# Two groups of maxima in every second step: a new order of TensorE's work in a two-layer attention and GLU kernel

## The chip, the cores and the metric

The kernel runs on one core of one Trainium2 chip. The metric is the time of one execution on the device in microseconds (us), the median over several runs. The profile is one further execution, recorded instruction by instruction. The engines are TensorE (PE, whose weight loads are listed apart as PEld), VectorE (DVE), ScalarE (ACT), GpSimd (POOL) and SyncE (SP, which issues most of the transfers).

## The reference

A sequence of 2048 rows of 448 numbers goes through attention, a GLU, attention and a GLU again, each with a layer norm ahead of it and a sum with its own input behind it. Both attentions use the same weights, and so do both GLUs.

```python
def _A_ref(x, wq, wk, wv, wo):
    B, S, D = x.shape
    H = 16
    Dh = D // H
    q = (x @ wq).reshape(B, S, H, Dh).transpose(0, 2, 1, 3)
    k = x @ wk
    v = x @ wv
    scores = jnp.einsum("bhqd,bkd->bhqk", q, k) * (Dh ** -0.5)
    p = _softmax(scores, axis=-1)
    o = jnp.einsum("bhqk,bkd->bhqd", p, v)
    ...
def _B_ref(x, w_gate, w_up, w_down):
    h = _sigmoid(x @ w_gate) * (x @ w_up)
    return h @ w_down
...
x = x + _A_ref(_layernorm(x, axis=-1), A_wq, A_wk, A_wv, A_wo)
x = x + _B_ref(_layernorm(x, axis=-1), B_w_gate, B_w_up, B_w_down)
```

(The einsums of the GLU are written as matrix products here.) All 16 heads of 28 numbers share one key and one value of 28 numbers per row. D is 448, the GLU's inner width F is 1792.

## The kernel before, in words

**Split numbers.** Most products are made in 16-bit numbers: a value is split into a high part and the rest, and three products (high with high, high with rest, rest with high) are added in PSUM. A product with 448 rows is so a chain of 11 matmuls (`chain`, line 338).

**Units and steps.** The queries are handled in units of 128 rows, 16 units per layer. For a unit all 16 heads are worked on together, and the keys are taken in 16 steps of 128 rows. A step (variable `kt`) has these parts:

- S, `scores` (line 507): one of four groups of four heads; a matmul (line 510) of 512 columns writes a bank of PSUM, and ScalarE takes the exponential into a tile P (line 513).
- P, `pv` (line 516): the products of a step's four P tiles with the values, in four column strips of the array at once, added up over the 16 steps in a bank of its own (line 521). P is made for the step before.
- M, one call of the generator `mx_gen` (line 464). It works for a later unit: it finds each query's largest score, which is subtracted inside the score product. A call makes four matmuls in four row strips of the array at once (line 480), each into a bank of its own, and VectorE reduces each of the four banks to a maximum (line 484). After sixteen groups, the next call first reduces the sixteen results (lines 493 and 494), has TensorE transpose them (`fin`, line 499), has VectorE copy them (line 501), and has GpSimd's queue store them into the tile QS with the queries (line 502); then it makes the next unit's first group.
- F, `fill.slice` (line 767): a slice of filler. The filler is a list of generators, each of which issues one matmul at a time with an assumed cost in ns: projections of queries (`qgen`, 11 x 216 per group of heads) and the GLU of blocks of two units (`Block.bulk`, line 651). A slice first runs the deferred work that is due (`flush`), then issues matmuls until its budget is spent.
- X: side work (`tick`, line 536): the stages of a finished unit (`Block.tile`, line 557: one over the sums of the softmax, by way of DRAM; the output product `wo`, line 612; the layer norm), and the setting of the filler's rate.

**The order.** It is written out by hand in the last loop: `ORDER = "FSFSFSFSPXM"` for each step. Engines take their work in the order in which it is issued. The rate per step is the filler that is left divided by the steps until it is due; the four slices share it.

**The GLU.** `glu(f)` (line 655) handles two blocks of 128 inner columns: 22 matmuls into the bank `gp`, from which ScalarE makes the tanh `th` (line 665; the sigmoid is written by a tanh); 22 into the bank `up`; then VectorE forms (th + 1) x up (line 673), ScalarE copies this in 16 bits as h (line 676), the GLU's second activation, and VectorE makes the rest (line 677). Seven such groups and two `down` products (line 692, 42 matmuls each) make a block.

**Deferral.** `defer(fn, lag)` (line 66) puts an evacuation off until a later `flush`; the lag counts slices. `fps` (line 80) takes a bank and flushes first.

**Banks and buffers.** Scores, maxima and every product of the filler take their banks from one pool of seven; the eighth bank is that of `pv`. Tiles of SBUF have a number of buffers each: P eight, the GLU's h `HB` = 10. Ahead of the main loop, the h buffers hold the rows of x as they are loaded (`load_x0`).

The functions that the change touches follow with their line numbers.

Of the kernel before, what the change touches and what calls it, by code (L numbers as in the profile page):

```python
# [19 lines left out]
def interleaved_layers_kernel(ctx: ExitStack, tc: tile.TileContext, x, wq, wk, wv, wo, wg, wu, wd, out, layers=2):  # L20
# [9 lines left out]
    H, Dh = 16, 28  # L30
    NT, NB, G, KT, FC = S // 128, S // 512, H // 4, S // 128, F // 128
    U = NT
    TB, WB, HB = 2, 4, 10
    NBL = NT // TB
    EPS = 1e-5

# [29 lines left out]
    def defer(fn, lag=0):  # L66

        pend.append((now[0] + lag, fn))

    def flush(every=False):  # L70
        todo, pend[:] = pend[:], []
        for i, (due, fn) in enumerate(todo):
            if due > now[0] and not every:
                pend.append((due, fn))
            else:
                fn()
        if every and pend:
            flush(True)
# [77 lines left out]
    def prep_q():  # L156
        parts = wk1.tile([128, 4], F32, name="parts", bufs=1)
        for c in range(4):
            junk = wk1.tile([128, D], F32, tag="P", name="junq", bufs=8)
            squares(parts[:, c:c + 1], rq[:, c], junk)  # L160
        nc.vector.tensor_reduce(mxa[:, 2:3], parts, axis=AX.X, op=OP.add)
        nc.vector.memset(WQ[:, :, :, :, Dh:32], 0.0)
        yield
        yield from scales(mxa[:, 2:3], 1, pwa[:, 2:3], swa[:, 2:3])
        for c in range(4):
            r = rq[:, c].rearrange("p (h d) -> p h d", d=Dh)
            split(WQ[:, 0, c, :, 0:Dh], WQ[:, 1, c, :, 0:Dh], r, swa[:, 2:3])
            yield
        nc.vector.tensor_scalar(esc, pwa[:, 2:3], pwa[:, 0:1], None, op0=OP.mult)
        nc.vector.tensor_scalar(esc, esc, Dh ** -0.5 * 2.0 ** -14, None, op0=OP.mult)  # L170
# [336 lines left out]
    def scores(l, u, kt, g, P):  # L507
        assert ("m", l, u) in stored, (l, u, kt)
        s = psf.tile([128, 512], F32, tag=BANKS["s"], name="s", bufs=NBK[BANKS["s"]])
        nc.tensor.matmul(s, KK[l][0:96, 0, kt * 128:(kt + 1) * 128], QS[l, u][:, g].rearrange("p h n -> p (h n)"),  # L510
                         start=True, stop=True)
        p = wk1.tile([128, 512], F32, tag="P", name="P", bufs=8)
        nc.scalar.activation(p, s, AF.Exp, scale=esc)  # L513
        P.append(p)

# [32 lines left out]
    class Block:  # L548
# [8 lines left out]
        def tile(self, u):  # L557

            l, b = self.l, self.b
            t = u % TB  # L560
            v = {}

            def f0():
                v["o"] = PVS.pop((l, u))
                nc.sync.dma_start(sums[u % 2], v["o"][28:128:32])
                v["xr"] = wk1.tile([128, D], F32, tag="xr", name="xr", bufs=4)
                nc.sync.dma_start(v["xr"], x[0, u * 128:(u + 1) * 128] if l == 0 else x2d[u])
                return
                yield

            def fx():
                v["rc"] = wk1.tile([128, 16], F32, name="rc")
                nc.sync.dma_start(v["rc"], sums[u % 2].rearrange("g (a b) -> (g a) b", b=16))
                return
                yield

            def fy():
                nc.vector.reciprocal(v["rc"], v["rc"])
                return
                yield  # L580

            def fz():
                nc.sync.dma_start(sums[u % 2].rearrange("g (a b) -> (g a) b", b=16), v["rc"])
                return
                yield

            def fw():
                lb = v["lb"] = wk1.tile([128, 512], F32, name="lb", bufs=1)
                for g in range(G):
                    nc.sync.dma_start(lb[32 * g:32 * g + 32], sums[u % 2][g:g + 1].to_broadcast([32, 512]))  # L590
                return
                yield

            def fa():
                nc.gpsimd.tensor_tensor(v["lb"], v["o"], v["lb"], op=OP.mult)  # L595
                return
                yield

            def fb():
                oT = v["oT"] = wk1.tile([128, 2, 512], F16, name="oT")  # L600
                nc.scalar.copy(oT[:, 0], v["lb"])
                defer(lambda: nc.vector.tensor_tensor(oT[:, 1], v["lb"], oT[:, 0], op=OP.subtract))  # L602
                return
                yield

            def fc():
                need(1)
                p = fps([128, D], F32, "wo")
                n = 0
                for h in range(4):  # L610
                    for a, c in ((0, 0), (0, 1), (1, 0)):
                        nc.tensor.matmul(p, v["oT"][:, a, h * 128:(h + 1) * 128], WO[:, c, h], start=n == 0, stop=n == 11)  # L612
                        n += 1
                        yield C448

                def f():
                    nc.vector.scalar_tensor_tensor(self.x1[:, t], p, osc, v["xr"], op0=OP.mult, op1=OP.add)
                    v["ls"] = ln_stats(self.x1[:, t])[0]
                defer(f)

            def fd():
                if t == TB - 1:
                    self.load_w(0)
                    self.load_w(1)
                v["hl"] = ln_split(self.x1[:, t], *v["ls"], eng=nc.gpsimd)
                return
                yield

            def fe():
                if t == 0:  # L630
                    self.XT2 = wk1.tile([128, 7, TB * 128], F16, name="XT2")
                t7_dma(v["hl"], self.XT2, t)
                return
                yield

            def ff():
                self.fed += 1
                if self.fed == TB:
                    fill.add(self.bulk(), BULK)
                    if b == NBL - 1 and not self.last:  # L640
                        fill.add(qgen(l + 1, 1), G * QCH)
                return
                yield
            return (1, f0), (1, fx), (1, fy), (1, fz), (1, fw), (1, fa), (1, fb), (2, fc), (2, fd), (3, fe), (2, ff)
# [6 lines left out]
        def bulk(self):  # L651
# [3 lines left out]
            def glu(f):  # L655

                for j in range(2):
                    if f + j + 2 < FC:
                        self.load_w(f + j + 2)
                w = [self.wt.pop(f + j) for j in range(2)]  # L660
                gp = fps([128, 2, TB * 128], F32, "gp")
                for j in range(2):
                    yield from chain(gp[:, j], lambda a, c, k: w[j][:k, 0, a, c], lambda c, k: XT2[:k, c], C256, True)
                th = wk1.tile([128, 512], F32, tag="s2", name="th", bufs=3)
                defer(lambda: nc.scalar.activation(th, gp.rearrange("p j n -> p (j n)"), AF.Tanh, scale=gsc))  # L665
                up = fps([128, 2, TB * 128], F32, "up")
                for j in range(2):
                    yield from chain(up[:, j], lambda a, c, k: w[j][:k, 1, a, c], lambda c, k: XT2[:k, c], C256, True)
                h = wk1.tile([128, 2, 512], F16, name="h", bufs=HB)

                def ev():
                    t = th
                    nc.vector.scalar_tensor_tensor(t, th, 1.0, up.rearrange("p j n -> p (j n)"), op0=OP.add, op1=OP.mult)  # L673

                    def parts():
                        nc.scalar.activation(h[:, 0], t, AF.Copy, scale=2.0 ** -17)  # L676
                        defer(lambda: nc.vector.scalar_tensor_tensor(h[:, 1], t, 2.0 ** -17, h[:, 0], op0=OP.mult,  # L677
                                                                     op1=OP.subtract), 1)
                    defer(parts, 2)
                defer(ev)  # L680
                hs.append(h)

# [215 lines left out]
        nmx += 1  # L898

    early[0] = False  # L900
    ORDER = "FSFSFSFSPXM"
    MORE = (5, 10)
    FIRST = KT * TB + 16
    KEEP = 28000
# [1 line left out]
    for l in range(layers):  # L906
# [10 lines left out]
        while late:  # L917
            late.pop(0)[1]()
        fill.slice(QCH)
        prevP = None  # L920
        rate = 0.0
        for step in range(U * KT):
            u, kt = divmod(step, KT)
            P = []
            for o in ORDER:
                if o == "S":
                    scores(l, u, kt, len(P), P)
                elif o == "M":
                    for _ in range(1 + (u == 0 and kt in MORE)):
                        next(mx, None)  # L930
                elif o == "P":
                    if prevP is not None:
                        pv(*prevP)
                elif o == "X":
                    if u and kt == 1:
                        b = (u - 1) // TB
# [9 lines left out]
                    else:  # L946
                        rate = max(fill.left - KEEP, 0) / (U * KT - step)
                else:
                    fill.slice(rate / ORDER.count("F"))
            prevP = (l, u, kt, P)  # L950
        pv(*prevP)
        flush(True)
        later(*BLK[l, NBL - 1].tile(U - 1))
        if not final:
# [33 lines left out]
```

## Time and profile before

| | |
|---|---|
| median of 3 runs | 2359.96 us (2359.76 to 2361.04) |
| the profiled execution's own time | 2358.22 us |
| its span, from the first to the last instruction | 2356.4 us |
| mean granted TensorE clock | 0.985 |
| PE, DVE, ACT, POOL busy | 2239.1, 1635.5, 1559.2, 336.8 us |

The span is the time between the first and the last instruction; the execution's own time is 1.8 us more. A row of the timeline begins with the start and the length in us from the span's start, then engine, line, operation, the tiles written and read, the shape and the count; the bracket at its end gives the idle time ahead of it and what ended it. A row of the groups gives the line, engine, operation, tiles, shapes and count, then busy us and the mean ns of one, then the idle time before them with its releasers. A matmul's length on PE holds its way through the array, so that the next one starts before it ends: what one costs is read from start to start.

### The profile page before, as it was taken

What the parts mean: (1) busy time and instruction counts of PE and PEld (TensorE: products, weight loads), DVE (VectorE), ACT (ScalarE), POOL (GpSimd) and SP (SyncE); (2) the same over time, 40 slices, a digit from 0 to 9 for tenths busy, and PEclk for the clock granted to TensorE, in tenths of its full rate; (3) what the DMA queues carried; (4) which work ended last, traced back from release to release, by engine and by line L of the source; (5) the groups of instructions that cost most, each with busy time, mean ns of one, the idle gap of its engine ahead of it and who ended that gap; (6) DMA issues with size and microseconds to landing.
All of it is one profiled execution on the core that took longest, in us unless ns stands there. A gap on an engine that the chain in (4) does not pass through costs nothing.

```text
span 2356.4 us, 41206 instructions
## 1 busy us (share of the span) xinstructions
PE 2239.1 (95%) x15736; PEld 1003.2 (43%) x15736; DVE 1635.5 (69%) x2917; ACT 1559.2 (66%) x2598; POOL 336.8 (14%) x602
## 2 busy tenths in 40 slices
PE   5888899999999999999998989999999999999999
PEld 3322243444444444444572224444444444444456
DVE  6888787777777777773358877867676777777321
ACT  5588676776667677677413777767676776767751
POOL 5203763100110110001101011000000000000010
PEclk9799999999999999999998999999999999999999
DMA  3244652323313132333342112222231313223133
GB/s 114 65 126 124 201 190 81 90 73 98 96 58 109 58 93 70 94 92 78 96 139 53 27 49 92 87 78 83 62 103 58 98 55 101 76 82 94 57 111 119
DMA packets 208071, 213.88 MB, mean 91 GB/s; under 512 B 139952, under 2 KB 168304, under 8 KB 207872
## 3 DMA queue, kind: packets, MB, share of 16 engines
q1 hardware_dynamic: 202496, 196.36, 28.5%
q0 software_dynamic: 5376, 14.87, 1.8%
q8 instruction: 123, 2.02, 0.4%
q14 instruction: 76, 0.62, 0.1%
HBM read 175.37 MB, written 23.59 MB: 84 GB/s over the span
## 4 chain that ended last, share of the span: by engine, by line
PE 51%; DVE 5%; DMA 1%; ACT 1%; issue 0%; SPq 0%; POOL 0%; ACTq 0%; DVEq 0%; POOLq 0%
PE pv L521 12%; PE s L510 10%; PE dn L702 8%; PE gp L345 7%; PE up L345 7%; DVE mp L484 4%; PE mx L480 4%; PE wo L612 2%; PE qp L345 1%; ACT P L513 0%; DMA sums<-rc 0%; DMA KK<-ktl 0%; DMA rc<-sums 0%; DMA sums<-pvs 0%; DVE st L297 0%
## 5 line engine op out<-in xcount | busy, mean ns | idle before, releaser
L513 ACT ACTIVATE P<-s,esc 128x512 f32<-128x512 f32 x2048 | 1307.8, 690 | 509.2 <-PE s L510 492.1
L484 DVE TENSOR_REDUCE mp<-mx 128x1 f32<-128x512 f32 x2048 | 1267.2, 681 | 412.2 <-PE mx L480 408.1
L510 PE MATMUL s<-QS,KK 96*128 96x512 f16 x2048 | 761.1, 381 | 52.7 <-DVE mp L484 34.8
L345 PEld LDWEIGHTS <-wgu 128*128 128x128 f16 x4928 | 458.6, 98 | 241.3 <-issue 94.5
L521 PE MATMUL pv<-P,VV 128*32 128x512 f32 x4096 | 547.3, 607 | 0.0
L345 PE MATMUL up<-XT,wgu 128*128 128x256 f16 x2464 | 375.6, 272 | 0.8 <-DVE mp L484 0.8
L345 PE MATMUL gp<-XT,wgu 128*128 128x256 f16 x2464 | 375.2, 274 | 0.2
L702 PE MATMUL dn<-WD,h 128*128 128x448 f16 x1344 | 321.7, 352 | 0.0
L510 PEld LDWEIGHTS <-KK 96*128 96x128 f16 x2048 | 194.5, 97 | 172.1 <-issue 93.0
L480 PE MATMUL mx<-KK,QH 32*128 32x512 f16 x2048 | 223.2, 392 | 20.7 <-ACT QH L402 4.8
L480 PEld LDWEIGHTS <-QH 32*128 32x128 f16 x2048 | 53.5, 91 | 396.5 <-issue 378.1
L702 PEld LDWEIGHTS <-h 128*128 128x128 f16 x1344 | 124.1, 98 | 136.6 <-issue 22.6
L521 PEld LDWEIGHTS pv<-P,VV 128*32 128x32 f32 x4096 | 80.9, 108 | 204.4 <-issue 192.6
L595 POOL TENSOR_TENSOR lb<-pvs,lb 128x512 f32<-128x512 f32 x32 | 40.5, 1265 | 800.3 <-DMA lb<-sums 679.4
L676 ACT ACTIVATE h<-th 128x512 f16<-128x512 f32 x112 | 70.2, 627 | 86.4 <-DVE th L673 86.3
L345 PE MATMUL qp<-XT,WQ 128*128 128x512 f16 x352 | 114.5, 403 | 3.8 <-DVE mp L484 2.4
L673 DVE SCALAR_TENSOR_TENSOR th<-th,up 128x512 f32<-128x512 f32 x112 | 75.8, 677 | 59.0 <-PE up L345 46.5
L303 POOL TENSOR_SCALAR rs<-mv 128x1 f32<-128x1 f32 (+2 forms) x53 | 13.6, 256 | 686.4 <-DVE mv L298 682.9
L677 DVE SCALAR_TENSOR_TENSOR h<-th,h 128x512 f16<-128x512 f32 x112 | 77.7, 693 | 46.7 <-ACT h L676 46.7
L665 ACT ACTIVATE th<-gp,gsc 128x512 f32<-128x512 f32 x112 | 76.8, 685 | 47.7 <-PE gp L345 47.7
L612 PE MATMUL wo<-WO,oT 128*128 128x448 f16 x384 | 78.4, 353 | 0.3 <-DVE oT L602 0.2
L345 PEld LDWEIGHTS <-WQ 128*128 128x128 f16 x352 | 34.2, 101 | 64.2 <-issue 41.1
(126 smaller groups left out, 834.3 us busy)
## 6 DMA issues: line engine op xcount, KB each, us to landing
wgu<-wgu_d SPq DMA_DIRECT2D x224, 512.0 KB
QS<-qd SPq DMA_DIRECT2D x384, 32.0 KB
lb<-sums SPq DMA_DIRECT2D x128, 64.0 KB
xr<-in_A_x_dram SPq DMA_DIRECT2D x32, 224.0 KB
qd<-qst POOLq DMA_DIRECT2D x28, 256.0 KB, 2.7
wgu_d<-sgu POOLq DMA_DIRECT2D x14, 512.0 KB, 3.8
QH<-qd SPq DMA_DIRECT2D x28, 128.0 KB
x2d<-x SPq DMA_DIRECT2D x16, 224.0 KB
```

The source lines that it names most:

```text
L345: nc.tensor.matmul(ps, a, b, start=n == 0, stop=n == 10)
L480: nc.tensor.matmul(ps[h], qh[32 * h:32 * h + 32, g], KK[l][32 * h:32 * h + 32, 1, kb * 512:(kb + 1) * 512], start=True, stop=True, tile_po ...
L484: nc.vector.tensor_reduce(mp[:, g, h, kb:kb + 1], ps[h], axis=AX.X, op=OP.max)
L510: nc.tensor.matmul(s, KK[l][0:96, 0, kt * 128:(kt + 1) * 128], QS[l, u][:, g].rearrange("p h n -> p (h n)"), start=True, stop=True)
L513: nc.scalar.activation(p, s, AF.Exp, scale=esc)
L521: nc.tensor.matmul(v[32 * g:32 * g + 32], VV[l][:, kt], P[g], start=kt == 0, stop=kt == KT - 1, tile_position=(0, 32 * g))
L612: nc.tensor.matmul(p, v["oT"][:, a, h * 128:(h + 1) * 128], WO[:, c, h], start=n == 0, stop=n == 11)
L665: defer(lambda: nc.scalar.activation(th, gp.rearrange("p j n -> p (j n)"), AF.Tanh, scale=gsc))
L673: nc.vector.scalar_tensor_tensor(t, th, 1.0, up.rearrange("p j n -> p (j n)"), op0=OP.add, op1=OP.mult)
L676: nc.scalar.activation(h[:, 0], t, AF.Copy, scale=2.0 ** -17)
L677: defer(lambda: nc.vector.scalar_tensor_tensor(h[:, 1], t, 2.0 ** -17, h[:, 0], op0=OP.mult, op1=OP.subtract), 1)
L702: nc.tensor.matmul(p, hs[f // 2][:, a, o:o + 128], WD[:, f, c], start=n == 0, stop=n == 3 * FC - 1)
```

## The change

From a unit's second on, and when the filler's rate is over 800 ns per step at the start of a pair of steps, the pair is issued as "FSFSMPMFSFSX" and "FSFSFSFSX": both steps' groups of maxima and the products of the two steps before it (P empties a list) stand in its first step. Otherwise the order stays "FSFSFSFSPXM". Each M is preceded by a flush. The GLU's second activation is put off by four slices and not by two. P has twelve buffers and not eight, h eight and not ten, and the 16-bit attention output oT one and not two.

```diff
-    TB, WB, HB = 2, 4, 10
+    TB, WB, HB = 2, 4, 8
...
-        p = wk1.tile([128, 512], F32, tag="P", name="P", bufs=8)
+        p = wk1.tile([128, 512], F32, tag="P", name="P", bufs=12)
...
-                oT = v["oT"] = wk1.tile([128, 2, 512], F16, name="oT")
+                oT = v["oT"] = wk1.tile([128, 2, 512], F16, name="oT", bufs=1)
...
-                    defer(parts, 2)
+                    defer(parts, 4)
...
-    ORDER = "FSFSFSFSPXM"
+    FULL = ("FSFSMPMFSFSX", "FSFSFSFSX")
+    POOR = ("FSFSFSFSPXM", "FSFSFSFSPXM")
+    ENOUGH = 800
...
-        prevP = None
+        pend_p = []
         rate = 0.0
         for step in range(U * KT):
             u, kt = divmod(step, KT)
             P = []
-            for o in ORDER:
+            if kt % 2 == 0:
+                pair = FULL if u and rate > ENOUGH else POOR
+            order = pair[kt % 2]
+            for o in order:
                 if o == "S":
                     scores(l, u, kt, len(P), P)
                 elif o == "M":
+                    flush()
                     for _ in range(1 + (u == 0 and kt in MORE)):
                         next(mx, None)
                 elif o == "P":
-                    if prevP is not None:
-                        pv(*prevP)
+                    while pend_p:
+                        pv(*pend_p.pop(0))
...
-                    fill.slice(rate / ORDER.count("F"))
-            prevP = (l, u, kt, P)
-        pv(*prevP)
+                    fill.slice(rate / order.count("F"))
+            pend_p.append((l, u, kt, P))
+        while pend_p:
+            pv(*pend_p.pop(0))
```

More of the change, by code (lines that the diff above doesn't have):

```diff
@@ L158, in prep_q @@
         for c in range(4):
-            junk = wk1.tile([128, D], F32, tag="P", name="junq", bufs=8)
+            junk = wk1.tile([128, D], F32, tag="P", name="junq", bufs=12)
             squares(parts[:, c:c + 1], rq[:, c], junk)
```

## The prediction

> **What bounds the kernel now.** I read the busy shares first, then two stretches of the busy time by window, then the groups of instructions, then single steps in the timeline. The page's first part:
>
> ```profile
> PE 2239.1 (95%) x15736; PEld 1003.2 (43%) x15736; DVE 1635.5 (69%) x2917; ACT 1559.2 (66%) x2598; POOL 336.8 (14%) x602
> ```
>
> PE is at 95%, but that is a mean. The busy time by window separates two stages of layer 1: the first units, with little filler, and a unit in which filler is plentiful.
>
> ```profile
> 1260.00:1320.00 60.00, 54.69 (x288) 14.16 (x290) 52.35 (x91) 36.71 (x62) 3.26 (x5) 0.94 0.06 18
> 1500.00:1565.40 65.40, 64.73 (x442) 26.80 (x440) 45.91 (x80) 44.14 (x70) 4.64 (x10) 1.00 0.22 64
> ```
>
> After the window and its length stand PE, PEld, DVE, ACT, POOL, the clock, the DMA share and GB/s. At 1260 DVE leads (52.35 of 60). At 1500 PE is busy 64.73 of 65.40 us, DVE 70%, ACT 67%: there the order on PE alone sets the time, and a gap on PE is lost. Part of one such step, to the filler behind a group of maxima (mx):
>
> ```profile
> 1506.24 0.38 PE L510 MATMUL s<-QS,KK 96*128 96x512 f16 x1
> 1506.46 0.49 PE L345 MATMUL up<-XT,wgu 128*128 128x256 f16 x3
> ...
> 1508.10 0.38 PE L510 MATMUL s<-QS,KK 96*128 96x512 f16 x1
> 1508.41 1.07 PE L521 MATMUL pv<-P,VV 128*32 128x512 f32 x8
> 1509.41 0.40 PE L480 MATMUL mx<-KK,QH 32*128 32x512 f16 x4
> 1509.74 0.61 PE L345 MATMUL up<-XT,wgu 128*128 128x256 f16 x4
> ```
>
> I call filler F, a score S, a step's products with the values P, a group of maxima M, and count from start to start: S to F 0.22 (1506.24 to 1506.46), S to P 0.31, P to M 1.00, M to F 0.33. S, S is 0.62 apart ((1508.10 - 1506.24) / 3). So S costs 0.09 more ahead of P than ahead of F, and M, as long as S in columns, 0.11 more: each change between full array, four column strips (P) and four row strips (M) costs about 0.1.
>
> **The change, part by part.** *Order.* A pair of steps is SP, PM, MF twice: 2 x (0.31 + 1.00 + 0.33) = 3.28. Now it has S to M, M to P, P to P, P to M, M to F, and one S to F more. P to P comes from its second half:
>
> ```profile
> 1677.19 0.61 PE L521 MATMUL pv<-P,VV 128*32 128x512 f32 x4
> 1677.73 0.40 PE L480 MATMUL mx<-KK,QH 32*128 32x512 f16 x4
> 1678.06 0.55 PE L702 MATMUL dn<-WD,h 128*128 128x448 f16 x2
> 1678.45 0.38 PE L510 MATMUL s<-QS,KK 96*128 96x512 f16 x1
> 1678.67 0.73 PE L702 MATMUL dn<-WD,h 128*128 128x448 f16 x3
> 1679.24 0.38 PE L510 MATMUL s<-QS,KK 96*128 96x512 f16 x1
> ...
> 1680.93 1.06 PE L521 MATMUL pv<-P,VV 128*32 128x512 f32 x8
> 1681.82 0.22 PE L499 MATMUL mt<-id,m 128*16 128x128 f16 x1
> ```
>
> The last four of P start 0.54 ahead of M, so the first half takes 1.00 - 0.54 = 0.46, and P ahead of P 0.92. S to M and M to P stand nowhere; without a switch they were 0.22 each, with two switches 0.42 each; I take the nearest rows, S to P 0.31 and M to F 0.33. New pair: 0.31 + 0.33 + 0.92 + 1.00 + 0.33 + 0.22 = 3.11. It saves 0.17 (0.37 to -0.03 by the bounds). The Trainium skill, "TensorE: Matmul & The Clock Gate", Single matmul latency, gives a warm matmul a fixed part of 398 cycles at 2.4 GHz; an estimate from that page is 0.17 us for a switch that hides none of it, so that by it M to P would be 0.07 dearer, 15 us in 208 pairs.
>
> How many pairs: the rate is the filler left over the steps left. With one block it is (14 x 22 x 110 + 2 x 42 x 190) / 32 = 1557, over 800; with only projections of queries (at most 28512 / 48 = 594) it is under. The first block is fed at the end of the third unit, so units 3 to 15 of both layers are filled: 2 x 13 x 8 = 208 pairs. 208 x 0.17 = **-35**.
>
> *Attention's output product* stands between P and M now:
>
> ```profile
> 1533.17 2.44 PE L612 MATMUL wo<-WO,oT 128*128 128x448 f16 x12
> 1535.54 0.40 PE L480 MATMUL mx<-KK,QH 32*128 32x512 f16 x4
> ```
>
> 2.37 for twelve: one more switch, 0.1. In a filled pair it stands behind S, before F, with none: 26 x 0.1 = **-3**.
>
> *The maxima's end.* Three groups are drawn ahead (one before unit 0, two extra in it), so the sixteenth group for the next unit is M of step 12. The call after it, step 13's, begins with the last reduction (m32, m16) and its transpose mt on PE. In the new order both are the two M of one pair. In between lie 0.33 + 0.92 + 0.89 (P to mt, 1680.93 to 1681.82) = 2.14. On DVE:
>
> ```profile
> 1678.15 2.48 DVE L484 TENSOR_REDUCE mp<-mx 128x1 f32<-128x512 f32 x4 [1.74 <-PE mx L480]
> 1680.55 0.67 DVE L710 SCALAR_TENSOR_TENSOR x<-dn,dsc,x 128x448 f32<-128x448 f32 x1
> 1681.14 0.21 DVE L493 TENSOR_REDUCE m<-mp 128x16 f32<-128x64 f32 x1
> 1681.38 0.17 DVE L494 TENSOR_SCALAR m<-m 128x16 f16<-128x16 f32 x1
> ```
>
> ```profile
> 947.03 0.17 DVE L494 TENSOR_SCALAR m<-m 128x16 f16<-128x16 f32 x1
> 947.26 0.09 PEld L499 LDWEIGHTS <-m 128*16 128x16 f16 x1 [1.20 <-DVE m L494]
> ```
>
> From M's start: 0.42 to the first reduction (1677.73 to 1678.15), 2.40 until the next operation starts, 0.24 for m32, then 0.23 from m16 to mt's weights: 3.29. PE waits 3.29 - 2.14 = 1.15, with everything behind it in its order. Units 3 to 14 of two layers: 24 x 1.15 = **+28**; with one of DVE's 0.67 us evacuations ahead of the group 24 x 1.8 = 43.
>
> *Banks.* Scores, maxima and filler share seven banks. That a full pool stops PE is shown in an early unit:
>
> ```profile
> 200.56 0.40 PE L480 MATMUL mx<-KK,QH 32*128 32x512 f16 x4
> 200.88 0.61 PE L510 MATMUL s<-QS,KK 96*128 96x512 f16 x2
> 201.73 0.70 PE L510 MATMUL s<-QS,KK 96*128 96x512 f16 x2 [0.24 <-DVE mp L484]
> ```
>
> ```profile
> 201.00 2.47 DVE L484 TENSOR_REDUCE mp<-mx 128x1 f32<-128x512 f32 x4
> ```
>
> Four banks of M, an open filler chain and two S make seven; the third S starts 0.11 after the first reduction's end (201.00 + 2.47 / 4 = 201.62). Now the new M1: it follows S2 by 0.31, and S1 by 0.93. ScalarE's rows:
>
> ```profile
> 1505.22 0.68 ACT L665 ACTIVATE th<-gp,gsc 128x512 f32<-128x512 f32 x1
> 1506.66 2.61 ACT L513 ACTIVATE P<-s,esc 128x512 f32<-128x512 f32 x4 [0.76 <-PE s L510]
> ```
>
> An exponential starts 0.42 after its S (1506.24 to 1506.66), follows another by 0.65 (2.61 / 4) and holds the bank until its end, 0.69 (the groups' row below). Set M1 at 0. S1's exponential ends at -0.93 + 0.42 + 0.69 = 0.18 at best, S2's later: both banks are taken, one holds the open chain, four are left, just what M1 needs. But eight S now come 0.62 apart from S3 of the pair before (start -4.65), and exponentials 0.65 apart: undisturbed S8's ends at -4.65 + 0.42 + 5 x 0.65 + 0.69 = -0.29. One other activation (0.65) among them makes that 0.36: M1's fourth matmul waits until 0.36 + 0.11, **0.45**. Two make it 1.01, and S7's 0.36: **1.1**. Before, P's 1.00 lay between S4 and M: S4's exponential ended 1.31 - 0.42 - 0.69 = 0.20 before M, and one running late left M five banks.
>
> How often: each GLU group of 44 matmuls puts th and h on ScalarE.
>
> ```profile
> L513 ACT ACTIVATE P<-s,esc 128x512 f32<-128x512 f32 x2048 | 1307.8, 690 | 509.2 <-PE s L510 492.1 <-PE gp L345 0.3 <-PE dn L702 0.2
> ...
> L665 ACT ACTIVATE th<-gp,gsc 128x512 f32<-128x512 f32 x112 | 76.8, 685 | 47.7 <-PE gp L345 47.7
> L673 DVE SCALAR_TENSOR_TENSOR th<-th,up 128x512 f32<-128x512 f32 x112 | 75.8, 677 | 59.0 <-PE up L345 46.5 <-ACT P L513 6.4 <-PE gp L345 6.1
> L676 ACT ACTIVATE h<-th 128x512 f16<-128x512 f32 x112 | 70.2, 627 | 86.4 <-DVE th L673 86.3
> ```
>
> With 1557 / 110 = 14 matmuls a step, gp and up (22 each) take 6.2 slices of F each. h is issued four slices after up's evacuation, so the next th follows it by about two: they fall into the same chain in six of the eight places, one alone in two. Mean (6 x 1.1 + 2 x 0.45) / 8 = 0.94 a group. Of the 112 groups 2 x 6 x 7 = 84 run beside maxima in filled pairs: 84 x 0.94 = 79. I take 0.85, as a slice may leave the next chain unopened: **+71**; bounds 0 (banks fall free in time) and 84 x 1.3 = 109 (a bank was bound ahead to the wrong tile). In the down product S come 0.79 apart (1678.45 to 1679.24), more than 0.65: nothing piles up, 0.
>
> *The rest at nothing:* h's later start is hidden while PE waits for nothing of it (its 86.3 us of waiting are ScalarE's own); twelve buffers for P are needed, not a gain; the flush before M only reorders DVE's work, within 5 us either way where DVE leads. Eight buffers ahead in the prologue:
>
> ```profile
> L794 SPq DMA_DIRECT2D xr<-in_A_x_dram x16: 327/405/594, 0.7 to 30.4; - x16
> L816 DVE BATCH_NORM_STATS2 st<-xr x16: 594/614/628, 3.3 to 43.2; 128x6 f32<-128x448 f32 x16
> ```
>
> The last load leads its use by 12.8; two tiles less (2 x 39.9 / 15 = 5.3) leave 7.5, and the first load needed 2.6. No cost, at most 5. *Queues:* a call of M also issues the next unit's loads (SP) and mr's store (POOL, busy 4.64 of 65.40). They now come up to a step earlier, and the stages of X on the other side of them; the next unit's scores read them two steps later or more, so nothing waits. Behind M1's waiting matmul stand P, P and all of PE's order; ScalarE and DVE go on with what they have, so a wait is not passed on to the next pair.
>
> **Sum.** -35 - 3 + 28 + 71 = +61 on the profiled run's 2358.2 us (span 2356.4): 2419. The runs' median lies 1.7 higher: **2421**.
>
> **Rivals.** A, the forecast, with its own range: banks 34 to 109, 2384 to 2460. The Trainium skill, "TensorEngine Tiling (Array Packing)", Restrictions and Gotchas, warns that row tiling raises PSUM pressure, since row tiles write different banks; the 0.24 us wait at 201.73 agrees.
> B, the faster side: banks fall free in time, because the flush ahead of M and the later h put th and h into ScalarE's gap behind M1. It decides where S8's exponential ends before M1, one activation less in the chain. Then -35 - 3 + 28 = -10: 2350. For it: ScalarE idles a third of the unit. Against: seven of the eight slices lie in or beside the chain.
> C: the transpose too finds DVE done: -38, 2322. Against it the 3.29 against 2.14.
> D: M to P and S to M cost two switches each, so the order saves nothing: 2421 + 35 = 2456.
> E: only double disturbances stop PE, half of the 71: 2386; or the change hardly bites, as few pairs exceed 800: 2360.
>
> **How the numbers follow.** A and the upper part of E 0.60, D 0.07, E's rest 0.08, B 0.20, C 0.05. Range 2345 to 2460: it takes in A, D, E and most of B, and leaves out C and the tails, 0.2. About 0.2% (4.7 us) is what a measurement here can tell from no change. Faster: most of B, and C, 0.24; same: 0.07; slower: 0.69.
>
> **What would show it.** In the filled units: P in groups of 16 matmuls, M to P near 0.33; once per unit a gap of about 1.15 before mt, put down to m (L494); gaps inside M's four matmuls of 0.4 to 1.1 put down to the exponential (L513), one or two per GLU group and none in the down product. If M's matmuls start without a gap, the bank term is wrong and the time is B's; if mt waits for nothing, C's. PE's busy share in filled units should fall from 99% to about 94%.

## The result and the profile after

The changed kernel takes 2393.27 us (median of 4 runs, 2391.18 to 2395.06), the kernel before 2359.86: a ratio of 1.0141, 95% interval 1.0123 to 1.0158. It is slower by 33 us; 61 were forecast, with a range of 2345 to 2460. The profiled execution's span is 2389.4 us (2356.4 before).

Busy time by window of the changed kernel, for the same two stretches as before (early units; one filled unit). The columns are the window, its length, PE, PEld, DVE, ACT, POOL, the clock, the DMA share and GB/s:

```profile
1260.00:1320.00 60.00, 52.36 (x273) 15.33 (x270) 49.59 (x88) 26.21 (x48) 6.61 (x13) 0.89 0.17 48
1505.90:1571.90 66.00, 63.88 (x468) 31.18 (x468) 48.58 (x83) 45.50 (x75) 4.94 (x10) 1.00 0.24 68
```

(The first window now holds the end of layer 0's tail, as everything is later by 19 us.) This filled unit takes 66.0 and not 65.4 us (in layer 1 the units now take 66.0 and 66.7 in turn), and PE is busy 63.88 of it, 97% where it was 99%. PE's instructions are the same; it waits more. The groups by line show where. First the kernel before, then the changed one; the columns are busy us and the mean ns of one, then the idle time ahead of them and what ended it:

```profile
L521 PE MATMUL pv<-P,VV 128*32 128x512 f32 x4096 | 547.3, 607 | 0.0
...
L480 PE MATMUL mx<-KK,QH 32*128 32x512 f16 x2048 | 223.2, 392 | 20.7 <-ACT QH L402 4.8 <-DMA KK<-ktl 4.6 <-DVE mp L484 4.1
```

```profile
L521 PE MATMUL pv<-P,VV 128*32 128x512 f32 x4096 | 511.9, 609 | 0.0
L480 PE MATMUL mx<-KK,QH 32*128 32x512 f16 x2048 | 271.0, 391 | 34.4 <-ACT P L513 7.9 <-DVE mp L484 5.1 <-ACT QH L402 4.8
```

The products P lose 35 us of busy time, because two groups now follow one another without a drain between them. The maxima M gain 48: their four matmuls, which started 3 ns apart, now often stand apart. A matmul here is drawn 0.39 long, so that a wait shorter than this inside a group shows as busy time and not as idle time; it must be read from start to start. (This is also why PE's busy share stands at 97% and not at the 94% that the prediction named as a sign.)

A pair without a wait, from the changed kernel's timeline of PE:

```profile
1527.46 0.38 PE L510 MATMUL s<-QS,KK 96*128 96x512 f16 x1
1527.78 0.39 PE L480 MATMUL mx<-KK,QH 32*128 32x512 f16 x4
1528.10 1.92 PE L521 MATMUL pv<-P,VV 128*32 128x512 f32 x16
1529.96 0.40 PE L480 MATMUL mx<-KK,QH 32*128 32x512 f16 x4
1530.29 0.61 PE L345 MATMUL gp<-XT,wgu 128*128 128x256 f16 x4
```

From start to start: S to M 0.32, M to P 0.32, both groups of P 1.86, M to F 0.33. With the extra S to F of 0.22 that is 3.05 against 3.28 before: 0.23 saved per pair, where 0.17 was forecast.

The transpose of the maxima, once a unit (PE's timeline, then VectorE's):

```profile
1568.49 0.40 PE L480 MATMUL mx<-KK,QH 32*128 32x512 f16 x4
1568.81 1.92 PE L521 MATMUL pv<-P,VV 128*32 128x512 f32 x16
1571.91 0.22 PE L499 MATMUL mt<-id,m 128*16 128x128 f16 x1 [1.18 <-DVE m L494]
```

```profile
1568.91 2.48 DVE L484 TENSOR_REDUCE mp<-mx 128x1 f32<-128x512 f32 x4 [1.51 <-PE mx L480]
1571.43 0.22 DVE L493 TENSOR_REDUCE m<-mp 128x16 f32<-128x64 f32 x1
1571.68 0.18 DVE L494 TENSOR_SCALAR m<-m 128x16 f16<-128x16 f32 x1
```

The transpose starts 3.42 after the unit's last group M, just behind the reductions; PE stands still for 1.18. In the 24 filled units with maxima the idle time ahead of the transpose is 1.05 to 1.39, 28.2 us in all; in the same units of the kernel before it is 2.8.

A pair in which M waits (PE's timeline, then ScalarE's):

```profile
1519.26 0.38 PE L510 MATMUL s<-QS,KK 96*128 96x512 f16 x1
1519.57 0.39 PE L480 MATMUL mx<-KK,QH 32*128 32x512 f16 x3
1520.15 0.37 PE L480 MATMUL mx<-KK,QH 32*128 32x512 f16 x1 [0.19 <-ACT th L665]
1520.45 1.93 PE L521 MATMUL pv<-P,VV 128*32 128x512 f32 x16
```

```profile
1515.36 2.49 ACT L513 ACTIVATE P<-s,esc 128x512 f32<-128x512 f32 x4 [2.30 <-PE s L510]
1517.75 0.62 ACT L676 ACTIVATE h<-th 128x512 f16<-128x512 f32 x1
1518.27 1.26 ACT L513 ACTIVATE P<-s,esc 128x512 f32<-128x512 f32 x2
1519.41 0.69 ACT L665 ACTIVATE th<-gp,gsc 128x512 f32<-128x512 f32 x1
1519.98 1.28 ACT L513 ACTIVATE P<-s,esc 128x512 f32<-128x512 f32 x2
```

Three matmuls of M start at 1519.57, the fourth 0.58 later, 0.05 after the tanh's end at 1520.10. On ScalarE h stands after the fourth of eight exponentials and th after the sixth, two slices apart, and the last two exponentials end only at 1521.26. I counted, at each waiting matmul of M in ten filled units of each layer, the banks between their first write and their last read: 133 matmuls in 103 of 320 groups waited, 51.0 us in all. At 114 of them, with 49.4 us, all seven banks were held. In the same units of the kernel before, three matmuls of M waited, 1.0 us in all.

### The profile page after: what moved, and what is told of

Its sections match the earlier page's. It is cut to its first block, busy times and chain, and to the rows that moved or that the text cites. A ratio compares the mean times of both kernels' runs of the same rounds, so it can differ in the third digit from the quotient of the medians.

```text
span 2389.4 us, 41472 instructions
## 1 busy us (share of the span) xinstructions
PE 2240.1 (94%) x15736; PEld 1048.5 (44%) x15736; DVE 1641.9 (69%) x2917; ACT 1530.9 (64%) x2598; POOL 338.9 (14%) x602
## 4 chain that ended last, share of the span: by engine, by line
PE 67%; DVE 14%; ACT 9%; issue 3%; DMA 2%; SPq 1%; POOL 1%; ACTq 0%; POOLq 0%; DVEq 0%
PE s L510 14%; PE pv L521 14%; PE dn L702 11%; DVE mp L484 10%; PE up L345 9%; PE gp L345 9%; ACT P L513 7%; PE mx L480 6%; PE wo L612 3%; PE qp L345 2%; DVE x L617 1%; DVE st L297 1%; ACT th L665 1%; ACT h L676 0%; DMA sums<-rc 0%
## 5 line engine op out<-in xcount | busy, mean ns | idle before, releaser
L513 ACT ACTIVATE P<-s,esc 128x512 f32<-128x512 f32 x2048 | 1290.3, 694 | 579.7 <-PE s L510 564.2
L345 PEld LDWEIGHTS <-wgu 128*128 128x128 f16 x4928 | 469.6, 98 | 222.4 <-issue 58.2
L521 PE MATMUL pv<-P,VV 128*32 128x512 f32 x4096 | 511.9, 609 | 0.0
L480 PE MATMUL mx<-KK,QH 32*128 32x512 f16 x2048 | 271.0, 391 | 34.4 <-ACT P L513 7.9
L510 PEld LDWEIGHTS <-KK 96*128 96x128 f16 x2048 | 196.3, 97 | 150.9 <-issue 66.7
L521 PEld LDWEIGHTS pv<-P,VV 128*32 128x32 f32 x4096 | 103.3, 109 | 280.0 <-issue 271.5
L617 DVE SCALAR_TENSOR_TENSOR x<-wo,osc,xr 128x448 f32<-128x448 f32 x32 | 21.9, 684 | 84.8 <-PE wo L612 84.8
## 6 DMA issues: line engine op xcount, KB each, us to landing
qd<-qst POOLq DMA_DIRECT2D x28, 256.0 KB, 2.6
```

The lines of the kernel that those rows point to most:

```text
L345: nc.tensor.matmul(ps, a, b, start=n == 0, stop=n == 10)
L480: nc.tensor.matmul(ps[h], qh[32 * h:32 * h + 32, g], KK[l][32 * h:32 * h + 32, 1, kb * 512:(kb + 1) * 512], start=True, stop=True, tile_po ...
L521: nc.tensor.matmul(v[32 * g:32 * g + 32], VV[l][:, kt], P[g], start=kt == 0, stop=kt == KT - 1, tile_position=(0, 32 * g))
```

## The experiments

The theory (T) is the prediction's: the order saves switches, and loses more to two new waits, the transpose's for VectorE and the first group's for a bank. Each ratio below is to the kernel before on the same chip, where its median was 2357.7 to 2360.2 us; a difference in us between two experiments is one of medians, and some of these were taken on different chips.

**1. The transpose one group later.**

```diff
-    LT = 1
+    LT = 2
```

> The changed kernel with one edit: the transpose of the maxima (L499) is issued one group of maxima later. Theory T (two new waits outweigh the saved mode switches: the transpose waits for VectorE, and the first group of maxima waits for PSUM banks): in the changed kernel's trace the idle time before the transpose in filled units is 1.05 to 1.18 us, 24 times; 22 of these go (the last unit of each layer has no later group), so 2393 - 26 = 2367. Rival R1 (the flush, the lag and the buffers cost the time, not the order): the wait was idle time that something else would have filled, 2393 within 5. Rival R2 (the long run of scores makes ScalarE late and the products wait for exponentials): within 5 of 2393 too.

Measured: 2365.82 us, ratio 1.0025 (1.0015 to 1.0034): 27.5 less than the changed kernel. In its timeline of PE the transpose stands at the head of the next pair's first group and waits for nothing:

```profile
1561.26 0.38 PE L510 MATMUL s<-QS,KK 96*128 96x512 f16 x1
1561.57 0.22 PE L499 MATMUL mt<-id,m 128*16 128x128 f16 x1
1561.73 0.40 PE L480 MATMUL mx<-KK,QH 32*128 32x512 f16 x4
```

The wait was worth its full length, as T has it; R1 and R2 expected no change. (The transpose of each layer's last unit still waits 1.18; the 22 waits that are gone make 25.8 us in the trace.) 5.6 us above the kernel before are left.

**2. A slice of filler ahead of the first group.**

```diff
-    FULL = ("FSFSMPMFSFSX", "FSFSFSFSX")
+    FULL = ("FSFSFMPMSFSX", "FSFSFSFSX")
```

> The changed kernel with one slice of filler moved from behind the pair's second group of maxima to ahead of its first (FSFSFMPMSFSX). The number of mode switches stays. T: ScalarE has 0.42 us more before the first group asks for four banks, so a single activation in the chain no longer stops it, and two stop it by 0.7 and not 1.1; the gaps inside the groups of maxima, 51 us in 20 units of the changed kernel (103 groups of 320), fall to a third: 2393 - 40 = 2353. R1: 2393 within 5, as flush, lag and buffers stay. R2: the run of eight scores stays, so the products would still wait: 2393 within 10.

Measured: 2385.82, ratio 1.0114 (1.0097 to 1.0131): 7.5 less, not 40. The direction is T's, the size is not. Counted from start to start in the same 20 units, the gaps in M fell from 51.0 to 35.6, and those ended by an exponential from 26.1 to 14.4. But the next score now followed the second group directly, 0.32 behind its start and without filler between, while the banks of M were held: start to start, the steps around it (M to S and S to F in place of M to F and F to S) grew by some 13 us. Seven banks were short at one place or at the other.

**3. The old order with the rest of the change.**

```diff
-    ENOUGH = 800
+    ENOUGH = 10 ** 9
```

> The changed kernel with the filled pairs switched off (the rate is never over the threshold), so that the order of the kernel before stands everywhere and only the flush before M, the longer lag and the numbers of buffers are left of the change. T: 2360 within 5. R1: near 2393. R2: 2360 within 5.

Measured: 2362.7, ratio 1.0016 (1.0007 to 1.0025). In the old order, flush, lag and buffers cost about 2.5 us (2 to 6 by the interval of the ratio); the rest of the 33 comes with the order. R1 falls.

**4. Both of 1 and 2.**

```diff
-    LT = 1
+    LT = 2
...
-    FULL = ("FSFSMPMFSFSX", "FSFSFSFSX")
+    FULL = ("FSFSFMPMSFSX", "FSFSFSFSX")
```

> Both edits: the transpose one group later and the filler slice ahead of the first group of maxima. T: the savings add up, 2393 - 26 - 40 = 2327, faster than the kernel before by 1.4%. R1 and R2: no faster than 2380.

Measured: 2369.02, ratio 1.0040 (1.0027 to 1.0053). No faster than experiment 1 alone: what the filler slice gained beside a waiting transpose it did not gain without it; why is not shown. My sum was wrong; the gain of 7.5 was not one that adds up.

**5. The second activation on GpSimd.** On top of experiment 1:

```diff
-                        nc.scalar.activation(h[:, 0], t, AF.Copy, scale=2.0 ** -17)
+                        nc.gpsimd.tensor_scalar(h[:, 0], t, 2.0 ** -17, None, op0=OP.mult)
...
-                                                                     op1=OP.subtract), 1)
+                                                                     op1=OP.subtract), 4)
```

> The kernel with the transpose one group later, and GLU's second activation (h) made by GpSimd and not ScalarE, its rest three slices later still. T (in a filled pair the first group of maxima finds all seven banks held, by exponentials that run late and by others): one of the two activations that delay the exponentials is gone; of the changed kernel's 51 us of gaps inside the groups of maxima in 20 filled units 26 were ended by an exponential and 8 by the tanh, and about half of these 34 should go: 2366 - 20 = 2346. Rival R3 (the gaps come from the exponentials' own number, eight scores in a row, whatever else ScalarE does): 2366 within 5.

Measured: 2344.11, ratio 0.9934 (0.9918 to 0.9951): 22 less than experiment 1, and faster than the kernel before. Its groups by line (the profiled execution took 2350.51 us):

```profile
L480 PE MATMUL mx<-KK,QH 32*128 32x512 f16 x2048 | 256.0, 393 | 26.7 <-DVE mp L484 5.9 <-ACT QH L402 4.8 <-DMA KK<-ktl 4.2
...
L676 POOL TENSOR_SCALAR h<-th 128x512 f16<-128x512 f32 x112 | 167.6, 1497 | 664.3 <-DVE th L673 663.0
```

GpSimd takes 1.5 us (its spans in the profile are rough) for what took ScalarE 0.63, but it has the time. M's busy time falls from 271.0 to 256.0 (experiment 1 alone left it at 270.4), and the counted gaps from 51.0 to 31.1; those ended by an exponential or the tanh are some 16 of these, where they were 34.5. The number of scores in a row is unchanged, so R3 falls: it matters what else ScalarE has between them. (The edit also puts h's rest off by three more slices; the two parts were not run one without the other.)

**6. Each step its own group, the products in pairs.**

```diff
-    FULL = ("FSFSMPMFSFSX", "FSFSFSFSX")
+    FULL = ("FSFSPMFSFSX", "FSFSMFSFSX")
```

> The changed kernel with the pair ordered FSFSPMFSFSX and FSFSMFSFSX: the products of two steps still stand together, but each step has its own group of maxima, half a pair apart. A pair then has five kinds of switches: S to P 0.31, P to P 0.41, P to M 0.525, M to F 0.317, S to M 0.313, M to F 0.317 = 2.19, where the order before has 2.30: -0.11 x 208 = -23. T: the transpose and its last group are nearly four us apart again, as before, so it does not wait; the first group follows two steps' products, 1.4 us after the last score, and finds its banks; the second follows two scores that came after a pause of ScalarE: few gaps, at most 10. 2360 - 23 + 5 = 2342. R3: the second group of maxima waits like the changed kernel's first: 2360 - 23 + 30 = 2367.

Measured: 2378.41, ratio 1.0082 (1.0067 to 1.0097). A miss, by two errors of mine in reading the order. From the first group to the second there is not half a pair but four scores with their filler:

```profile
1554.12 0.39 PE L480 MATMUL mx<-KK,QH 32*128 32x512 f16 x4
...
1557.20 0.38 PE L510 MATMUL s<-QS,KK 96*128 96x512 f16 x1
1558.02 0.22 PE L499 MATMUL mt<-id,m 128*16 128x128 f16 x1 [0.43 <-DVE m L494]
```

From 1557.20 the next group could start 0.31 later, 3.4 after 1554.12, which is too soon for the reductions: the transpose still waits, by 0.43 and 0.88 in turn in layer 1 and by 1.1 to 1.3 in most filled units of layer 0, 20.6 us in all against the changed kernel's 28.2. And the second group follows four scores, not two, so it lacks banks (37.7 us of counted gaps in 20 units, against 51.0), while the first, behind the products, waits nowhere. R3's number is the nearer one: its second group waits, and the transpose's waits, which it did not have, come on top.

**7 and 8. Six banks.** The same edit in the changed kernel and in the kernel before:

```diff
-    NBK = {"f": 7, "s": 2, "m": 3}
+    NBK = {"f": 6, "s": 2, "m": 3}
```

> The changed kernel with six banks for scores, maxima and filler and not seven. T: now even an undisturbed pair lacks a bank when its first group asks for four (two scores, one chain), and waits some 0.3 us for an exponential; disturbed pairs wait for one exponential more (0.65): 190 pairs x 0.4 = 76 more, 2393 + 76 = 2469, nearly all of it as gaps inside groups of maxima. If banks were not what the gaps are for: 2393 within 10.

> The kernel before with six banks. T: a group of maxima follows the products there, when the scores' banks have come free, so that the filled units lose little (under 5 us in all); the early units of a layer, where VectorE leads, lose at most 15: 2360 + 10 = 2370. If any bank less costs every order the same: as much as the changed kernel loses.

Measured, one run each: 2521.96 for the changed kernel (129 more) and 2470.72 for the kernel before (111 more). I expected the old order to lose a tenth of that, and it does not. Groups by line, first the changed kernel with six banks, then the kernel before with six:

```profile
L510 PE MATMUL s<-QS,KK 96*128 96x512 f16 x2048 | 765.9, 381 | 74.7 <-DVE mp L484 47.5 <-ACT P L513 23.3 <-DVE x L617 1.8
...
L480 PE MATMUL mx<-KK,QH 32*128 32x512 f16 x2048 | 332.3, 392 | 61.8 <-ACT P L513 35.6 <-DVE mp L484 6.3 <-ACT th L665 4.0
```

```profile
L510 PE MATMUL s<-QS,KK 96*128 96x512 f16 x2048 | 767.5, 382 | 109.4 <-DVE mp L484 88.0 <-ACT P L513 14.5 <-DVE ktl L376 2.1
...
L480 PE MATMUL mx<-KK,QH 32*128 32x512 f16 x2048 | 240.7, 395 | 24.9 <-DVE mp L484 8.0 <-DMA QH<-qd 4.4 <-DMA KK<-ktl 3.8
```

The old order, too, lives on all seven, but is short at another place: its scores behind M wait for the reductions (88.0 us), while the new order's M wait for the exponentials (busy 332.3, idle ahead of it 61.8). Counted in the 20 units, the gaps inside M grew from 51 to 119 us in the new order and from 1 to 13 in the old one. The pair of runs supports that banks are what M waits for; it does not show that the old order has a bank to spare.

**9. The lag back at two**, in the changed kernel.

```diff
-                    defer(parts, 4)
+                    defer(parts, 2)
```

> The changed kernel with the second activation's lag back at two slices. T: the activation is then issued while VectorE is still at the reductions ahead of its product, so ScalarE stands still for it and the exponentials behind it are later: more gaps inside the groups of maxima, 2393 + 15 = 2408. R1 (the longer lag is part of the loss): 2380 or less.

Measured: 2403.93, ratio 1.0195 (1.0179 to 1.0210), 10.7 more (13 by the two ratios). The waits of ScalarE, first of the changed kernel, then of this one, in total us, times and the longest:

```profile
ACT h L676 <- DVE th L673: 44.7, 19, 3.2
```

```profile
ACT h L676 <- DVE th L673: 74.9, 43, 9.3
```

Counted start to start, the gaps in the first groups grew from 45.9 to 54.8 us in the 20 units, as T has it. The longer lag is a gain inside the new order; R1 falls again.

**10. The control: the second activation on GpSimd in the old order.** Its order is unchanged.

```diff
-                        nc.scalar.activation(h[:, 0], t, AF.Copy, scale=2.0 ** -17)
+                        nc.gpsimd.tensor_scalar(h[:, 0], t, 2.0 ** -17, None, op0=OP.mult)
...
-                                                                     op1=OP.subtract), 1)
-                    defer(parts, 2)
+                                                                     op1=OP.subtract), 4)
+                    defer(parts, 4)
```

> Control: the kernel before, its order unchanged, with GLU's second activation on GpSimd and the longer lags. T: in the filled units of the kernel before no group of maxima waits for a bank, so a lighter ScalarE gains nothing: 2360 within 4. If the second activation's move is a gain by itself (R4), as much as it gained in the new order: 2360 - 22 = 2338.

Measured: 2352.84, ratio 0.9975 (0.9966 to 0.9985). A gain of 6 where I expected none within 4, and far from R4's 22. So about 16 of experiment 5's 22 belong to the new order. Counted from transpose to transpose, the filled units give 0.35 and 0.21 us each in the two layers, some 7 in all. From start to start, 4 of the 6 us in 20 units lie between a filler matmul and the score behind it; a score that waits less for its bank would do that, but this is not shown.

**11. All three edits.** On top of experiment 5:

```diff
-    FULL = ("FSFSMPMFSFSX", "FSFSFSFSX")
+    FULL = ("FSFSFMPMSFSX", "FSFSFSFSX")
```

> The transpose later, the second activation on GpSimd, and the slice of filler ahead of the first group of maxima. T: the filler slice took 15 of 51 us of gaps at the first group and gave half of that back at the score behind the second; with fewer gaps left (31 us in 20 units) it can take at most 6: 2344 - 4 = 2340, the same within 5.

Measured: 2346.82, ratio 0.9957 (0.9940 to 0.9973): the same as experiment 5 within the intervals.

**12. The later transpose in filled pairs alone.** On top of experiment 5:

```diff
-    LT = 2
+    LT = [1]
...
-            late.append([LT, fin])
+            late.append([LT[0], fin])
...
+                LT[0] = 2 if pair is FULL else 1
```

Its reason is a row of the waits of experiment 1 (total us, times, longest):

```profile
PE s L510 <- DMA QS<-mr: 5.9, 4, 2.0
```

> The kernel with the later transpose and the second activation on GpSimd, where the transpose is put off only in filled pairs. Putting it off everywhere made four scores in the early units wait 5.9 us in all for the transposed maxima's transfer (DMA QS<-mr); early units have the old place back. T: 2344 - 6 = 2338, 0.9% faster than the kernel before. If those waits were covered by VectorE's lead in the early units: 2344 within 3.

Measured: 2346.29, ratio 0.9948 (0.9934 to 0.9961): no gain over experiment 5. The number is that of the second case, but its reason is not what the traces show. PE's waits, first of experiment 5, then of this one:

```profile
PE s L510 <- DMA QS<-mr: 5.8, 4, 2.0
...
PE mt L499 <- DVE m L494: 2.4, 2, 1.2
```

```profile
PE mt L499 <- DVE m L494: 7.1, 9, 2.1
...
PE s L510 <- DMA QS<-mr: 2.5, 2, 2.0
```

The scores wait 3.3 us less for the transfer, and the early units' transposes, back in their old place, wait 4.7 us more for VectorE: the wait moved from the score to the transpose.

## Why the prediction was right, point by point

The forecast was slower by 61; it is slower by 33, for the two reasons given: experiment 1 takes the first away, experiment 5 lessens the second and experiment 7 enlarges it. The terms:

| term | forecast | measured | from |
|---|---|---|---|
| order of the pair | -35 | -48 | 208 x 0.23 from the timeline |
| output product | -3 | -3 | S to the product and on to S, both without a switch |
| transpose | +28 | +27.5 | experiment 1 (idle time: 28.2, of which 2.8 stood there before) |
| banks | +71 | +61 | 51.0 counted in 20 units, for 24 |
| scores behind M | 0 | about -10 | F to S start to start, 0.3 to 0.6 a unit sooner |
| flush, lag, buffers | 0 | +2.5 | experiment 3 |

The measured terms sum to +30 of +33; about 3 are not assigned. That the sum for the banks came near 71 is in part luck, as its parts below show.

- *The switches* were costed from the nearest rows. M to P, which stood nowhere, is 0.30 in most pairs (1520.15 to 1520.45) and at times 0.32: 0.08 to 0.1 above the 0.22 without a switch. By the estimate from the Trainium skill, "TensorE: Matmul & The Clock Gate", Single matmul latency, it would have been 0.17 above; the measurement decides for the row. The two groups of P were forecast as 0.92 + 1.00 and are 1.86.
- *The transpose* waits 1.17 or 1.18 in most filled units with maxima (1.05 to 1.39) where 1.15 was worked out.
- *The banks* are the step whose size was off, and by more inside than the sum says. Exponentials and tanh end 34.5 us of the gaps in 20 units, 41 in 24, or 0.49 per GLU group, not 0.85. The term that was too large is the wait of a disturbed pair. I sorted the pairs without an output product by what ScalarE started between 4.3 us ahead of the first group and 0.3 behind its start: the 40 with both th and h all waited, by 0.59 in the mean and not 1.1; of 16 with one of them, 10 waited, 0.26 in the mean of the 16 and not 0.45. That is 40 such pairs for 70 GLU groups, where six of eight were forecast. In the down product next to nothing piled up (0.6 us in 38 pairs), as forecast. In their place others hold banks that I had put at nothing: the output product (8.0, ten times 0.4 in each layer: it uses up the filler's budget, so that two scores and the group follow it at once, before VectorE has read its bank), the next layer's keys (2.9), and the reductions of the first group, for which the second waits (5.4). Five pairs of layer 0 without th or h waited 1.3 each; a cast of the next layer's norm (L314) stood on ScalarE in that time, which the forecast did not have. The rule of "TensorEngine Tiling (Array Packing)" in the Trainium skill, Restrictions and Gotchas, that row tiling raises PSUM pressure, agrees with the 114 waits at seven held banks.
- *Scores behind M* waited for reductions in the kernel before (9.2 and 7.4 us of idle time in the filled stretches of the two layers). In the new order these waits are fewer (4.2 and 4.9). I had not counted a wait of before that would go.
- *The prologue and the queues* were put at nothing. Experiment 3 holds the prologue's buffers, within its 2.5. The queues' part comes with the order: in the changed kernel PE waits 4.1 us for a load of QH, 4.0 before, and no score waits for the transposed maxima.
- *Rival B* (2350) needed the banks to come free in time; experiment 5 partly made that so and gave 2344, with the transpose's wait gone as well. *Rival C* falls by the 1.18. *Rival D* falls by the 0.30 to 0.32. *Rival E*'s 2386 is nearer to 2393 than the forecast's 2421, and in part for its reason: the pairs with two activations hold 23.6 us of the gaps in 20 units, those with one 4.1; but single disturbances do stop PE, and the other causes above are not in it.

## What to carry to other kernels

Grouping work of one array mode saves about 0.1 us per switch, but it also bunches the consumers: count the banks that each group asks for at once against those that are still waiting to be read. Before moving a group, look for the one call in sixteen that reads the result of its neighbour; here it cost 28 us of a 48 us gain, and a delay by one group gave it back. When a pool is full, shifting the order moves the wait to another place (experiments 2 and 6); taking work off the engine that frees the pool lessened it here (experiment 5: 51.0 to 31.1 us of gaps).

## What the runs showed of the hardware

At a granted clock of 1.00 each change of TensorE's mode cost about the same, 0.08 to 0.12 us, whichever two modes. From the full array it was 0.09 to column strips (S to P 0.31, where S to F takes 0.22) and 0.1 to row strips (S to M 0.31 to 0.32). From row strips it was 0.1 to the full array (M to F 0.32 to 0.33) and 0.08 to 0.1 to column strips (M to P 0.30 to 0.32). From column to row strips it was 0.12: the last four products start 0.55 ahead of M, where four follow four after 0.43. Two groups of column-strip products in a row show none: the step from one to the other is 0.43 too. GpSimd scaled 128 x 512 numbers from 32 to 16 bits in 1.5 us beside a VectorE busy 74% of a filled unit (47.34 of 64.20 us in experiment 5's busy time by window), and VectorE's own operations stayed as long as they were (h's second part 688 ns against 706).
